# Attention loads reordered: v ahead of q and k, raw weights later, q scaled later in a round

## The chip, the cores and the metric

The kernel runs on one core of one Trainium2 chip. The metric is device time in microseconds (us), the median of several runs. The engines are TensorE (PE in the profile, its weight loads PEld), VectorE (DVE), ScalarE (ACT), GpSimd (POOL) and SyncE (SP), whose queue (SPq) issues every load and store here. Times in the profile count from the start of the profiled span.

## The reference, cut to what matters

Three stages follow one another: sparse attention over 4 batches and 8 heads, and two feed-forward layers on its output.

```python
# q, k, v: (4, 8, 576, 64)
scores = q @ k.T / 8
local   = (rel >= 0) & (rel < 32)                    # heads 0 to 3
strided = (rel >= 0) & (pos_k % 32 == pos_q % 32)    # heads 4 to 7
attn = softmax(where(mask, scores, -1e9))
x = (attn @ v)             # to (2304, 512)
h = x @ w_in               # (512, 2048)
x = (h * cos(h)) @ w_out   # (2048, 512)
x = (silu(x @ w_gate) * (x @ w_val)) @ w_out2        # d_ff 1536
```

The weights arrive in a wide type: a raw tile of 128 x 512 values is 512 KB and has to be converted to float32 (ACT and DVE) and scanned for its largest magnitude before it is split into two half-precision parts.

## The kernel before

Attention works on 16 units (a batch and a pair of heads), two at a time, one strided and one local. A unit has three groups of tiles; the groups of two units alternate, so a **round** of six steps treats two units, and the loop at L775 runs over steps k with i = 2 (k // 6) and g = k % 6. There are 48 groups and eight rounds. Group j has its scores and row maxima in step j (L784, L785), its exponentials one step later (L814, on ACT), its row sums (DVE) and its normalisation (`norm`, L456: a reciprocal on DVE, then a product on POOL) in step j + 2, its transposes and their evacuation in step j + 5 (PE, then ACT), its product with v in step j + 6 (`values`, L479) and its store into the activations in step j + 7 (`put`).

Each engine takes its instructions in the order in which the program emits them. In each step `pump` (L815) adds about one us of work on the weights, from step 5 on: a raw tile is widened on ACT (`g0`, L224), scanned (`g1`, L227), shifted (`g2`, L231) and completed on DVE (`g3`, L235). The first call of `pump`, in step 5, emits `g0` of raw tiles 0 and 1 on ACT ahead of everything of step 6, and `g0` of tile 2 follows in step 6. The freed tile is loaded again by `load_raw` (L158) with the next one of a fixed order: 16 tiles of w_in, then w_out. There are six raw buffers.

All loads stand in one queue, SP's. Ahead of the loop (L737 to L754) it holds q and k of units 0 and 1, four small constants, v of units 0 and 1, and then raw tiles mixed with q and k of units 2 to 5 and v of units 2 and 3. Inside the loop, in step g = 5 of a round, it gets q and k of the units three rounds on (L808) and then v of the next round (L812). q and k lie in one tile, and v of a strided unit is loaded by two transfers of 54 partitions (L408), of a local unit by one of 96 (L404).

q has to be scaled in place before the scores of its unit. That is `scale_q` (L413), one POOL instruction for each unit; it waits for the load of that unit's q and k, and all later POOL instructions stand behind it. It is emitted for the two units of the next round in steps g = 2 and g = 3 (L786), ahead of the step's `norm`. PE emits a small extra product (L437) in each group, on ones.

After the loop, the first layer starts (L1012) and works on with the converted weights; its own weight work is again emitted between its products.

Of the kernel before, what the change touches and what calls it, by code (L numbers as in the profile page):

```python
# [55 lines left out]
HEAD, HSHARE = 14, 0.8  # L56
RATE, MINLAG = 0.4, 2
RAW = 6
XM = 5
HOMES, LATE, UNIT = 24, 4, 16  # L60
W7S = 3
# [10 lines left out]
def is_local(p):  # L72
    return p < NPAIR // 2
# [6 lines left out]
def build(tc, qk_l, qk_s, v_l, v_s, w_in, w_out, w_gate, w_val, w_out2, mask_l, mask_s, eye32, eye16, out):  # L80
    nc = tc.nc
    wide = w_in.dtype != F32
    with ExitStack() as ctx:
# [65 lines left out]
        for k, a in MATS.items():  # L149
# [3 lines left out]
        order = deque([("in", j) for j in range(M1)] + [("out", j) for j in range(M1)] * 2  # L153
                      + [(mat, j) for mat in ("gate", "val") for j in range(M2)]
                      + [(mat, 2 * j + i) for j in range(NPR) for mat in ("gate", "val") for i in range(2)]
                      + [("out2", j) for j in range(M2)] * 2)

        def load_raw():  # L158
            if not order:
                return  # L160
            mat, i = order.popleft()
            src = MATS[mat][i]
            if wide:
                t = ring.tile([128, 512, 2], I32, name="raw", bufs=RAW)
                nc.sync.dma_start(out=t.rearrange("p n w -> p (n w)"), in_=src.bitcast(I32))
            else:
                t = ring.tile([128, 512], F32, name="raw", bufs=RAW)
                nc.sync.dma_start(out=t, in_=src)
            raw.setdefault((mat, i), deque()).append(t)
# [20 lines left out]
        def pump(share):  # L190

            credit[0] = min(credit[0] + share, max(share, 1.0))
            while fill and credit[0] > 0:
                step_fill()

        def need(key):
            while key not in emitted:
                step_fill()
# [191 lines left out]
        units = [(b, p) for b in range(NB) for p in (2, 0, 3, 1)]  # L390
        qk_t, v_t = {}, {}

        def load_qk(i):
            b, p = units[i]
            loc = is_local(p)
            qk_t[i] = ap.tile([128, QKW[loc]], F32, name="qkl" if loc else "qks", bufs=3)
            nc.sync.dma_start(out=qk_t[i], in_=(qk_l if loc else qk_s)[b, p % 2])

        def load_v(i):
            b, p = units[i]  # L400
            loc = is_local(p)
            if loc:
                v_t[i] = ap.tile([LW, LT, 128], F32, name="vl")
                nc.sync.dma_start(out=v_t[i], in_=v_l[b, p % 2])  # L404
            else:
                v_t[i] = v_pair[i // 2 % 2]
                for u in range(2):
                    nc.sync.dma_start(out=v_t[i][64 * u:64 * u + SW, SP * u:SP * u + SP, :], in_=v_s[b, p % 2, u])  # L408

        def bank():  # L410
            return pm.tile([128, 512], F32, name="bank")

        def scale_q(i):  # L413
            q = qk_t[i][:, 0:S if is_local(units[i][1]) else QP]
            nc.gpsimd.tensor_scalar(out=q, in0=q, scalar1=SCALE, scalar2=1.0, op0=ALU.mult, op1=ALU.mult)
# [145 lines left out]
        def up1(blk, m, ks=range(KC), c=None, spare=None):  # L561
            n = BLOCKS[blk][1]
            if m == 0 and not c:
                turn[blk] = prod(sx[blk][1], scale_w["in"][1], 1.0 / TWO_PI)
            if not c:
                b = bank() if spare is None else pacc.tile([128, 512], F32, name=f"acc{spare}")
                c = dict(n=n, ph=b[:, 0:n], blk=blk)
            project(c["ph"], wi[m], xs[blk], n, ks)
            return c

        def up1_a(c):
            n = c["n"]
            c["w"] = ring.tile([128, 512], F32, name="tb", bufs=4)[:, 0:n]
            nc.scalar.activation(out=c["w"].bitcast(I32), in_=c["ph"], func=AF.Identity, scale=turn[c["blk"]], bias=quarter)  # L574
# [27 lines left out]
        def fold_pieces(blk, scales, dst, spans):  # L602
            n = BLOCKS[blk][1]
            h = n // 2
            y = xy[blk]
            b11, b12, b21, b22 = (y[:, k:k + 2, t:t + h] for k in (0, 2) for t in (0, h))
            t1, t2 = (t.rearrange("p (k n) -> p k n", k=2)[:, :, 0:h] for t in spans)
            parts = [(0, b11), (1, b21), (2, b22), (4, t1), (5, t2), (6, t1), (3, t2)]

            def sub(out, a, b):  # L610
                nc.vector.tensor_tensor(out=out, in0=a, in1=b, op=ALU.subtract)

            sums = {0: lambda: sub(t1, b12, b11), 1: lambda: sub(t2, b22, t1), 5: lambda: sub(t1, b22, b12),
                    6: lambda: sub(t2, b21, t2)}

            def piece(k):
                if k == 0:
                    dst[blk] = ring.tile([128, 2, 7, 512], F16, name="xs")
                hl = [dst[blk][:, i].rearrange("p q (k n) -> p q k n", k=2)[:, :, :, 0:h] for i in range(2)]
                s = scales[blk][0]  # L620
                if k in sums:
                    sums[k]()
                if k < 7:
                    i, src = parts[k]
                    hi_part(hl[0][:, i], src, s)
                if k:
                    i, src = parts[k - 1]
                    lo_part(hl[1][:, i], src, s, hl[0][:, i])
            for k in range(8):
                yield (0.7 if k else 0) + (0.7 if k in sums else 0), lambda k=k: piece(k)  # L630
# [107 lines left out]
        load_qk(1)  # L738
        for t, a in ((id16, eye16), (ms, mask_s), (ml, mask_l), (id32, eye32)):
            nc.sync.dma_start(out=t, in_=a)  # L740
        load_v(0)
        load_v(1)
        load_raw()
        load_qk(2)
        load_raw()
        load_qk(3)
        load_raw()
        load_v(2)
# [2 lines left out]
        load_qk(4)  # L751
        load_raw()
        load_qk(5)
        load_raw()  # L754
        warm = bank()
        for _ in range(WARM):
            nc.tensor.matmul(out=warm, lhsT=ones16, rhs=hot, start=True, stop=True)
# [13 lines left out]
        def keep_warm():  # L771
            t = bank()[:, 0:4 * LW].rearrange("p (n w) -> p n w", w=LW)
            nc.tensor.matmul(out=t, lhsT=id16, rhs=ml, start=True, stop=True)

        for k in range(len(gs) + LAGS[3] + 1):  # L775
            def group(lag):
                return gs[k - lag] if 0 <= k - lag < len(gs) else None
            i, g = 2 * (k // 6), k % 6
            if group(LAGS[0]):
                group(LAGS[0]).sums()  # L780
            if group(LAGS[1]):
                group(LAGS[1]).transposes()
            if group(0):
                group(0).scores()  # L784
                group(0).top()  # L785
                if g in (2, 3) and i + g < len(units):  # L786
                    scale_q(i + g)
            begun = k - len(gs) - K0
            if 0 <= begun < 2 * EARLY:
                m = begun // 2  # L790
                if begun % 2 == 0:
                    need(("in", m))
                    early = up1(0, m, range(KC // 2))
                else:
                    up1(0, m, range(KC // 2, KC), early)
                    up1_a(early)
                    steps.append((0, m, early))
            elif not group(0):
                keep_warm()
            if group(LAGS[3]):  # L800
                group(LAGS[3]).put()
            if group(LAGS[1]):
                group(LAGS[1]).evac()
            if group(LAGS[2]):
                group(LAGS[2]).values()
            if group(0) and g == 5:
                for j in (i + 6, i + 7):
                    if j < len(units):  # L808
                        load_qk(j)
                for j in (i + 2, i + 3):  # L810
                    if i and j < len(units):
                        load_v(j)  # L812
            if group(1):
                group(1).exps()  # L814
            pump(PUMP if k >= KP else 0)  # L815
            if group(LAGS[0]):
                group(LAGS[0]).norm()

        attn.close()
        pacc = ctx.enter_context(tc.tile_pool(name="pacc", bufs=1, space=bass.MemoryType.PSUM))  # L820
# [149 lines left out]
        def urge(pieces, key=None):  # L970
            urgent.extend((c, f, key) for c, f in pieces)
# [40 lines left out]
        for blk in range(NBLK):  # L1012
            for m in range(M1):
# [6 lines left out]
                if m == 0:  # L1020
                    if blk:
                        need_urgent(("xs", blk))
                    if blk == NBLK - 1:
                        urge(fold_pieces(0, sy, ys, spans), ("ys", 0))
                if m == (2 if blk else XM) and blk + 1 < NBLK:
                    urge(scale_pieces(blk + 1, sx))
# [135 lines left out]
        for s, (blk, j) in enumerate(slots):  # L1162
            n = BLOCKS[blk][1]
            h = n // 2
            if s == 1:
                need(("out2", NPR - 1))
                for _ in range(RAW):
                    t = ring.tile([128, 512, 2] if wide else [128, 512], I32 if wide else F32, name="raw", bufs=RAW)
                    flat = t.rearrange("p n w -> p (n w)") if wide else t
# [152 lines left out]
```

## Time and profile before

| quantity | value |
|---|---|
| median of 3 runs | 902.8 us (899.58 to 903.82) |
| span of the profiled execution | 902.2 us |
| mean granted clock of TensorE | 0.979 |
| PE busy | 862.4 us (96%) |
| DVE busy | 691.8 us (77%) |
| ACT busy | 521.2 us (58%) |
| POOL busy | 199.3 us (22%) |

The profiled execution took its span, 902.2 us; nothing is shown around it. The attention loop takes about the first 113 us. A share of busy time is a mean over stages with different limits, so the stages are read one by one. In a timeline row the first two numbers are start and duration, and the bracket at its end gives the idle time before the first of its instructions and what ended it. A row with x12 merges twelve instructions. The granted clock is a share of full speed: 1.00 is 2.4 GHz and 0.50 is 1.2 GHz.

### The profile page before, as it was taken

How to read it: one execution, taken by the hardware profiler on the slowest of the kernel's cores; microseconds unless marked ns; L12 is line 12 of the kernel's file. 1: busy time of each engine (PE TensorE's matmuls, PEld its weight loads, DVE VectorE, ACT ScalarE, POOL GpSimd, SP SyncE). 2: the span in 40 equal slices, each digit the busy share in tenths (PEclk: the TensorE clock that was granted, in tenths of full speed). 3: DMA queues.
4: the chain of work that ended last, by engine and by line, in shares of the span. 5: the costliest groups of instructions: out<-in, count | busy, mean ns of one | idle time of the engine just before them, and what ended most of it. 6: DMA issues, size and time to landing. Idle time of an engine off the chain costs nothing.

```text
span 902.2 us, 18542 instructions
## 1 busy us (share of the span) xinstructions
PE 862.4 (96%) x7228; PEld 609.8 (68%) x7228; DVE 691.8 (77%) x1337; ACT 521.2 (58%) x1046; POOL 199.3 (22%) x253
## 2 busy tenths in 40 slices
PE   7999999989999979899999998899999999999998
PEld 4776644434444434455655686788888899999998
DVE  4797989896758999869988378857886776776672
ACT  4787988763445667547887355536444444544440
POOL 3342414121234656522322200000000000000000
PEclk8897999999999989999999999999999999999999
DMA  9997751568545675651645344657677687888894
GB/s 302 352 304 219 249 187 48 163 189 272 191 144 197 214 241 178 225 204 49 215 136 198 156 151 177 247 200 265 233 255 267 216 273 284 299 290 309 317 330 148
DMA packets 53512, 200.61 MB, mean 222 GB/s; under 512 B 5456, under 2 KB 16208, under 8 KB 49584
## 3 DMA queue, kind: packets, MB, share of 16 engines
q1 hardware_dynamic: 53424, 199.42, 64.8%
q8 instruction: 57, 0.93, 0.5%
q14 instruction: 31, 0.25, 0.1%
HBM read 175.41 MB, written 23.99 MB: 221 GB/s over the span
## 4 chain that ended last, share of the span: by engine, by line
PE 66%; DVE 10%; ACT 7%; DMA 6%; issue 6%; POOL 4%; SPq 0%; POOLq 0%; ACTq 0%; DVEq 0%
PE acc L693 14%; PE bank L541 10%; PE bank L543 10%; PE bank L542 10%; PE acc L541 5%; PE acc L543 5%; PE acc L542 5%; DMA vl<-v_l 3%; PE bank L435 2%; DVE arena L248 2%; POOL arena L915 2%; POOL arena L589 2%; PE po L488 2%; ACT arena L245 2%; DMA v_pair<-v_s 1%
## 5 line engine op out<-in xcount | busy, mean ns | idle before, releaser
L541 PE MATMUL bank<-xs,wi 128*128 128x256 f16 (+3 forms) x780 | 233.8, 300 | 22.1 <-DVE tb L584 9.1
L543 PE MATMUL bank<-xs,wi 128*128 128x256 f16 (+3 forms) x780 | 234.1, 300 | 0.0
L542 PE MATMUL bank<-xs,wi 128*128 128x256 f16 (+3 forms) x780 | 233.9, 300 | 0.0
L589 POOL TENSOR_TENSOR arena<-tb,arena 128x512 f16<-128x512 f32 (+1 forms) x80 | 91.7, 1148 | 240.6 <-ACT arena L588 205.7
L542 PEld LDWEIGHTS <-wi 128*128 128x128 f16 x880 | 86.2, 98 | 62.5 <-issue 30.2
L541 PE MATMUL acc<-arena 128*128 128x512 f16 (+1 forms) x320 | 114.7, 358 | 0.0
L542 PE MATMUL acc<-arena 128*128 128x512 f16 (+1 forms) x320 | 114.5, 358 | 0.0
L543 PE MATMUL acc<-arena 128*128 128x512 f16 (+1 forms) x320 | 114.5, 358 | 0.0
L541 PEld LDWEIGHTS <-wi 128*128 128x128 f16 x880 | 86.3, 98 | 38.4 <-issue 4.1
L543 PEld LDWEIGHTS <-wi 128*128 128x128 f16 x880 | 86.3, 98 | 35.6 <-issue 1.4
L693 PEld LDWEIGHTS <-arena 128*128 128x128 f16 x1080 | 100.7, 98 | 8.2
L678 POOL TENSOR_TENSOR wi<-tb 128x256 f32<-128x256 f32 (+1 forms) x30 | 20.2, 675 | 347.5 <-DVE tb L659 347.5
L663 ACT ACTIVATE arena<-tb 128x256 f16<-128x256 f32 (+3 forms) x59 | 28.9, 489 | 115.3 <-DVE tb L659 111.6
L574 ACT ACTIVATE tb<-bank,quarter,c 128x512 int32<-128x512 f32 (+1 forms) x75 | 54.4, 725 | 49.5 <-PE bank L543 36.9
L542 PEld LDWEIGHTS <-arena 128*128 128x128 f16 x600 | 58.8, 98 | 35.0 <-issue 2.5
L693 PE MATMUL acc<-arena 128*128 128x256 f16 (+1 forms) x702 | 82.0, 265 | 0.0
L543 PEld LDWEIGHTS <-arena 128*128 128x128 f16 x600 | 58.7, 98 | 33.0 <-issue 0.2
L541 PEld LDWEIGHTS <-arena 128*128 128x128 f16 x600 | 58.8, 98 | 32.8 <-ACT arena L588 0.3
L658 DVE SCALAR_TENSOR_TENSOR tb<-tb,arena 128x512 f32<-128x512 f32 (+1 forms) x60 | 38.0, 634 | 44.9 <-ACT tb L652 44.8
L588 ACT ACTIVATE arena<-tb 128x512 f16<-128x512 f32 (+1 forms) x80 | 46.5, 581 | 35.4 <-PE acc L543 32.4
L541 PE MATMUL bank<-xs,arena 128*128 128x256 f16 (+1 forms) x240 | 62.9, 262 | 1.7 <-DVE arena L1190 1.2
L543 PE MATMUL bank<-xs,arena 128*128 128x256 f16 (+1 forms) x240 | 62.9, 262 | 0.0
(146 smaller groups left out, 1734.5 us busy)
## 6 DMA issues: line engine op xcount, KB each, us to landing
wi<-w SPq DMA_DIRECT2D x20, 1792.0 KB
arena<-w SPq DMA_DIRECT2D x60, 576.0 KB, 5.3
raw<-w_out SPq DMA_DIRECT2D x56, 512.0 KB, 4.0
arena<-w SPq DMA_DIRECT2D x10, 1792.0 KB
raw<-w_gate SPq DMA_DIRECT2D x24, 512.0 KB, 4.6
raw<-w_val SPq DMA_DIRECT2D x24, 512.0 KB, 4.4
w<-arena SPq DMA_DIRECT2D x42, 256.0 KB, 2.1
raw<-w_in SPq DMA_DIRECT2D x16, 512.0 KB
```

Of the source, the lines that this page charges most:

```text
L245: nc.scalar.activation(out=dst, in_=src, func=AF.Copy, scale=s)
L248: nc.vector.scalar_tensor_tensor(out=dst, in0=src, scalar=s, in1=hi, op0=ALU.mult, op1=ALU.subtract)
L541: nc.tensor.matmul(out=o, lhsT=w[:, 0, c], rhs=x[0], start=first, stop=False, **kw)
L542: nc.tensor.matmul(out=o, lhsT=w[:, 0, c], rhs=x[1], start=False, stop=False, **kw)
L543: nc.tensor.matmul(out=o, lhsT=w[:, 1, c], rhs=x[0], start=False, stop=last, **kw)
L574: nc.scalar.activation(out=c["w"].bitcast(I32), in_=c["ph"], func=AF.Identity, scale=turn[c["blk"]], bias=quarter)
L588: nc.scalar.activation(out=g[:, 0, 0:n], in_=w, func=AF.Copy)
L589: nc.gpsimd.tensor_tensor(out=g[:, 1, 0:n], in0=w, in1=g[:, 0, 0:n], op=ALU.subtract)
L658: nc.vector.scalar_tensor_tensor(out=t, in0=t, scalar=1.0, in1=gate, op0=ALU.add, op1=ALU.mult)
L663: nc.scalar.activation(out=to, in_=src, func=AF.Copy, scale=2.0 ** -11)
L678: nc.gpsimd.tensor_tensor(out=t_sums[:, 0, 0:h], in0=c["t"][0][:, h:2 * h], in1=c["t"][0][:, 0:h], op=ALU.subtract)
L693: nc.tensor.matmul(out=o[:, c], lhsT=w[:, 256 * i + 128 * c:256 * i + 128 * c + 128], rhs=unit(u)[:, x:x + h], start=j == c == i == 0, sto ...
```

## The change

Four edits, all in the attention stage.

- `scale_q` for the next round moves from steps g = 2 and 3, ahead of `norm`, to the end of steps g = 4 and 5, behind `norm`.
- In step g = 5 the loads of v for the next round are issued ahead of those of q and k for three rounds on.
- In the loads ahead of the loop, q and k of unit 2 come ahead of v of units 0 and 1, and the raw tiles come later: the first stands behind q and k of unit 3 and three at the very end. Their number (six) is the same.
- `load_raw` holds back any w_out tile; from step 30 on, each step releases one, until none is held, and then loads go out as before.

```diff
--- before.py
+++ after.py
@@ -56,6 +56,7 @@
 HEAD, HSHARE = 14, 0.8
 RATE, MINLAG = 0.4, 2
 RAW = 6
+RELEASE = 30
 XM = 5
 HOMES, LATE, UNIT = 24, 4, 16
 W7S = 3
@@ -155,7 +156,22 @@
                       + [(mat, 2 * j + i) for j in range(NPR) for mat in ("gate", "val") for i in range(2)]
                       + [("out2", j) for j in range(M2)] * 2)
 
+        hold, held_back = [True], [0]
+
+        def release():
+            if held_back[0]:
+                held_back[0] -= 1
+                next_raw()
+            else:
+                hold[0] = False
+
         def load_raw():
+            if hold[0] and order[0][0] == "out":
+                held_back[0] += 1
+            else:
+                next_raw()
+
+        def next_raw():
             if not order:
                 return
             mat, i = order.popleft()
@@ -738,11 +754,9 @@
         load_qk(1)
         for t, a in ((id16, eye16), (ms, mask_s), (ml, mask_l), (id32, eye32)):
             nc.sync.dma_start(out=t, in_=a)
+        load_qk(2)
         load_v(0)
         load_v(1)
-        load_raw()
-        load_qk(2)
-        load_raw()
         load_qk(3)
         load_raw()
         load_v(2)
@@ -751,7 +765,8 @@
         load_qk(4)
         load_raw()
         load_qk(5)
-        load_raw()
+        for _ in range(3):
+            load_raw()
         warm = bank()
         for _ in range(WARM):
             nc.tensor.matmul(out=warm, lhsT=ones16, rhs=hot, start=True, stop=True)
@@ -783,8 +798,6 @@
             if group(0):
                 group(0).scores()
                 group(0).top()
-                if g in (2, 3) and i + g < len(units):
-                    scale_q(i + g)
             begun = k - len(gs) - K0
             if 0 <= begun < 2 * EARLY:
                 m = begun // 2
@@ -804,17 +817,21 @@
             if group(LAGS[2]):
                 group(LAGS[2]).values()
             if group(0) and g == 5:
+                for j in (i + 2, i + 3):
+                    if i and j < len(units):
+                        load_v(j)
                 for j in (i + 6, i + 7):
                     if j < len(units):
                         load_qk(j)
-                for j in (i + 2, i + 3):
-                    if i and j < len(units):
-                        load_v(j)
             if group(1):
                 group(1).exps()
             pump(PUMP if k >= KP else 0)
             if group(LAGS[0]):
                 group(LAGS[0]).norm()
+            if group(0) and g >= 4 and i + g - 2 < len(units):
+                scale_q(i + g - 2)
+            if k >= RELEASE:
+                release()
 
         attn.close()
         pacc = ctx.enter_context(tc.tile_pool(name="pacc", bufs=1, space=bass.MemoryType.PSUM))
```

## Rows read from the trace of the kernel before

**Rows 1.** The page's slices of the span, 40 equal ones: granted clock and DMA share.

```profile
PEclk8897999999999989999999999999999999999999
DMA  9997751568545675651645344657677687888894
```

**Rows 2.** Busy time by stage: stretch, PE, PEld, DVE, ACT, POOL, clock, DMA share, GB/s.

```profile
14.50:31.00 16.50, 15.98 (x149) 10.81 (x149) 8.66 (x23) 10.18 (x33) 5.47 (x10) 0.51 1.03 361
...
31.00:60.00 29.00, 29.00 (x491) 20.89 (x491) 27.43 (x76) 26.91 (x103) 12.94 (x20) 1.00 1.00 310
...
72.50:82.20 9.70, 9.70 (x96) 6.67 (x96) 4.98 (x13) 5.90 (x20) 2.51 (x4) 0.51 0.60 188
...
128.00:160.00 32.00, 31.82 (x150) 14.39 (x149) 30.32 (x57) 27.54 (x45) 13.64 (x13) 1.00 0.17 58
```

**Rows 3.** Timeline of POOL in the opening.

```profile
6.28 0.67 POOL L415 TENSOR_SCALAR qkl<-qkl 128x576 f32<-128x576 f32 x1 [0.80 <-DMA qkl<-qk_l]
13.32 0.69 POOL L415 TENSOR_SCALAR qks<-qks 128x594 f32<-128x594 f32 x1 [6.37 <-DMA qks<-qk_s]
```

**Rows 4.** Timeline of PE in the opening, the transposes of group 0.

```profile
14.57 0.69 PE L470 MATMUL tp<-id,e_s 128*128 128x128 f32 x2 [3.38 <-POOL e_s L459]
```

**Rows 5.** Timeline of ACT in the opening.

```profile
16.15 1.24 ACT L224 ACTIVATE wi<-raw 128x512 f32<-128x512 f32 x2
18.31 0.49 ACT L477 ACTIVATE pt<-tp 96x384 f32<-96x384 f32 x1 [0.92 <-PE tp L466]
```

**Rows 6.** The page's list of DMA issues, sizes of one transfer.

```profile
raw<-w_in SPq DMA_DIRECT2D x16, 512.0 KB
...
qks<-qk_s SPq DMA_DIRECT2D x8, 594.0 KB, 6.6
...
vl<-v_l SPq DMA_DIRECT2D x8, 432.0 KB, 4.7
...
v_pair<-v_s SPq DMA_DIRECT2D x16, 162.0 KB
```

**Rows 7.** Busy time, columns as in rows 2, of two stretches with different loads.

```profile
36.00:38.50 2.50, 2.50 (x40) 1.69 (x37) 2.40 (x6) 2.28 (x9) 0.46 (x1) 1.00 1.02 410
40.00:43.00 3.00, 3.00 (x47) 2.03 (x47) 2.97 (x7) 2.70 (x12) 2.37 (x3) 1.00 0.99 228
```

**Rows 8.** The chain that ended last: start, duration, what.

```profile
58.90 12.35 DMA v_pair<-v_s
```

**Rows 9.** Timeline of PE: scores and products with v, at either clock.

```profile
47.62 0.71 PE L435 MATMUL bank<-qkl 64*64 64x96 f32 x12
...
53.36 0.56 PE L435 MATMUL bank<-qks 64*64 64x54 f32 x12
...
71.29 0.56 PE L488 MATMUL po<-pts,v_pair 118*64 118x54 f32 x12 [0.79 <-DMA v_pair<-v_s]
...
72.40 1.23 PE L435 MATMUL bank<-qkl 64*64 64x96 f32 x12
...
82.17 0.56 PE L435 MATMUL bank<-qks 64*64 64x54 f32 x12
```

**Rows 10.** Timelines of POOL (`norm` in g = 4) and PE (scores in g = 0).

```profile
33.57 0.55 POOL L459 TENSOR_TENSOR e_s<-e_s,ls 128x216 f32<-128x216 f32 x1 [1.32 <-DVE ls L458]
...
96.25 0.55 POOL L459 TENSOR_TENSOR e_s<-e_s,ls 128x216 f32<-128x216 f32 x1 [1.17 <-ACT xy L510]
...
34.60 0.67 PE L435 MATMUL bank<-qks 64*64 64x54 f32 x16
...
96.89 0.67 PE L435 MATMUL bank<-qks 64*64 64x54 f32 x16
```

**Rows 11.** Busy time, columns as in rows 2, ahead of the second fall of the clock.

```profile
68.40:71.80 3.40, 2.19 (x38) 1.54 (x38) 3.15 (x8) 3.00 (x9) 1.09 (x2) 1.00 1.03 258
```

**Rows 12.** The raw tiles until 130 us: duration min/median/max, first and last start.

```profile
L165 SPq DMA_DIRECT2D raw<-w_out x22: 327/328/447, 55.6 to 126.1; - x22
...
L174 DVE TENSOR_REDUCE pw_out<-raw x16: 662/677/682, 90.8 to 125.4; 128x1 f32<-128x512 f32 x16
```

## Prediction

> **What bounds the kernel now.** I read the slices first, then busy time by stage, then the timelines around each place where the clock fell. In the slices the reader sees a busy PE nearly throughout, and TensorE's granted clock low in two places of the attention stage; the DMA engines are full for some 70 us and then ease [rows 1]. By stage, PE is busy all of 31 to 60 us at full clock with DVE at 27.43 of 29 us, so attention there goes at PE's pace with DVE close behind; behind attention, at 128 to 160 us, PE is busy 31.82 of 32 us and DMA has room [rows 2]. So time won in attention should come off the end nearly whole. What can be won lies in the two stretches at half clock, 14.5 to 31 and 72.5 to 82.2 us, where DVE and ACT wait for PE [rows 2].
>
> Each begins at a wait for a load. In the opening, POOL stands 6.37 us at the `scale_q` of unit 2, until its q and k land at 13.32 [rows 3]. `norm` of group 0 stands behind it, and PE, at the transposes of that group, is idle for 3.38 us and restarts at 14.57 [rows 4], at half clock. At 71.29 PE waits 0.79 us for v of unit 8 [rows 9], a load that took 12.35 us from issue, to 71.25 [rows 8]; then the clock falls again.
>
> **Term 1, v ahead of q and k.** In step g = 5 of round 3, v of units 8 and 9 stood behind q and k of units 12 and 13, and behind one w_out tile, issued at 55.6 us [rows 12]; the change takes both from ahead of it. A q and k pair is two tiles of some 594 KB, 1.21 MB, a raw tile 0.52 MB [rows 6]. Such loads run at 410 GB/s, against 228 GB/s in a stretch that mostly moves v [rows 7]. So v lands 1.21/0.410 + 0.52/0.410 = 4.2 us earlier, five times the 0.79 us that PE waited. In round 4 it gains as much or more. q and k then land later, but they are loaded three rounds, some 33 us, before their scores, so nothing is late for that.
>
> What goes if v is there: PE's scores of step 31 began at 72.40. From the products at 71.29, less 0.79 of wait, and with the transposes between them at full clock, they could begin near 71.15, which is 1.25 us earlier. Steps 31 to 34 then took 82.17 - 72.40 = 9.77 us; the same three steps two rounds earlier at full clock took 53.36 - 47.62 = 5.74 us [rows 9], so half clock cost 4.0 us. Together 5.2 us. Next late would be ACT, some 0.4 us ahead of the same products, which stays. Bounds: 1.2 us if the clock falls here all the same, 5.2 if not; I take 5.2, because 4.2 us of lead is far from the wait.
>
> The Trainium skill, "TensorE: Matmul & The Clock Gate", section Terms, prices throttled time at one minus the clock's share: half of these 9.77 us would be 4.9 us. The rows give 4.0, since the steps did not quite halve in speed, so the measurement decides; by the page the total would be 0.9 us better.
>
> **Term 2, the opening.** q and k of unit 1 are there at 6.28 [rows 3]. The sum of the loads from there, with 0.6 us for the constants, 3.4 us for a pair of v (0.77 MB at 228), 1.48 us for a q and k tile and 1.28 us for a raw tile (both at 410) [rows 6, 7], gives for unit 2 before: 6.28 + 0.6 + 3.4 + 1.28 + 1.48 = 13.0, and the row says 13.32 [rows 3]. The same sum for the new order: q and k of unit 2 at 8.4, v of units 0 and 1 at 11.8, q and k of unit 3 at 13.2, raw tile 0 at 14.5, v of units 2 and 3 at 17.9, raw tile 1 at 19.2, raw tile 2 at 22.0. So POOL no longer blocks `norm`, and PE's transposes of group 0 come at about 11.8 instead of 14.57.
>
> But there is a new wait. In step 5 ACT gets the widening of raw tiles 0 and 1, done at 17.39 before, and the evacuation of group 1 stands behind them, at 18.31 [rows 5]. With tile 1 landing at 19.2, or 0.5 us later if v runs slower, the widening ends at 19.9 to 20.4 and the evacuation at about 20.9; PE's product of group 1 waits for it. DVE's scan of tile 0 waits too, and through its reciprocal `norm` and then `scale_q` of unit 3 come at about 17.8, which holds PE's scores of step 7. So the 3.4 us of idle time at one place becomes some 5 us in three or four pieces, and step 8 begins at about 21.9 where it began at 24.35 before (14.57 plus three steps of 9.77/3 = 3.26 us). That is 2.4 us ahead. What it is worth depends on the clock. Before, the half clock held 16.5 us from the restart, the second time 9.8 us. Restarting at 21.0, it would hold to 37.5 or to 31.7. In the first case 15.6 us at 3.26 bring PE to step 12.8, which it reached at 31.0 + 2.8 x 1.91 = 36.3 before, 1.2 us earlier; in the second it is at step 11 at 31.7, against 32.8 before, 1.1 us won. If the clock never falls, ACT limits the gain to 3.3 us, because it has the delayed widenings to do and is busy 26.91 of 29 us anyway [rows 2]. So the bounds are a loss of 1.2 and a gain of 3.3. I take 0: gaps this long have brought the clock down before, and the two hold times lie on either side.
>
> **Term 3, q scaled later.** Before, the scaling came three or four steps ahead of its scores and cost nothing after the opening. Now it stands behind `norm` of step g = 4, and PE needs it two steps later. `norm` waits for a reciprocal that DVE reaches only after that step's row maxima and weight work. On the trace of before, `norm` of that step in round 1 starts at 33.57 and takes 0.55; with 0.69 for the scaling [rows 3] it would be done at 34.81, and PE wants the scores at 34.60: 0.21 us late. In round 6 it is 96.25 + 1.24 = 97.49 against 96.89, 0.60 late [rows 10]. The six rounds 1 to 6 come to 2.2 us (0.21 and 0.60 are the first and the last). The other unit's scaling, one step later, has the same distance; as the first wait has already put PE back, it mostly hides. Bounds: 0.5 us, if DVE, given time by each wait, loses its lag; 4.4 us, if the second scaling costs as much again. I take 2.2, straight from the rows.
>
> **Term 4, w_out held back.** The held tiles go out from step 30, near 70 us; the first scan of w_out stands at 90.8 us [rows 12], near 86 after the other terms. Three tiles take 3.8 us at 410 GB/s, and the queue by then is shorter by what was taken off it. Nothing: the cover is some 12 us, and without it each tile would cost 1.3 us. The new order adds no instruction; SP's queue has no new wait except that v's buffer is freed a little later in a step than that of q and k, which then stand behind v.
>
> **Sum.** 902.2 - 5.2 + 0 + 2.2 = 899.2 us on the profiled execution; the median of the runs stands 0.6 us above that execution, so 899.8 us.
>
> **The rivals.** A, the opening keeps its clock or gets it back soon: +3.3 us of gain, and with `scale_q` costing 1 us rather than 2.2 the time is 899.8 - 4.5 = 895.3 us. For it: PE restarts early, with shorter gaps than 3.38 us. Against it: several of them together.
>
> B, slower: the new waits for `scale_q` bring the clock down in the middle of attention. For it: before the second fall PE was busy 2.19 of 3.40 us [rows 11], so 1.2 us of idle time stood ahead of it; a round in which both scalings are late by 0.6 us each looks the same. The price of one fall is 4.0 us (three steps, as above) to 6.8 (16.5 us in steps of 3.26 instead of 1.91 us): 903.8 to 906.6 us for one fall, 907.8 to 913 us for two. It decides from the second fall on. Against it: most of the waits by the rows are below 0.6 us.
>
> The same page of the Trainium skill (section on why this matters for kernels) lets the clock fall after a gap in which PE does nothing, and by it waits of half a microsecond would never cost it, so rival B would have next to no chance. The trace disagrees: PE was busy for most of the stretch before the fall [rows 11].
>
> C, the change doesn't do what it says: the stage is bound by the loads, PE meets another late load instead, and terms 1 and 3 fall away together, as a scaling hides in a load's wait: 902.8 us. For it: DMA is full to 70 us [rows 1, 2]. Against it: v's new place is 4.2 us ahead, and all that is held back can wait.
>
> **How the numbers follow.** The forecast, 899.8 (896.5 to 902.5), has 0.45; A has 0.22; B 0.23, of which 0.12 for one fall and 0.11 for two; C 0.10. What a measurement can tell from no change is about 0.5%, 4.5 us, so faster means below 898.3. A lies there, and 0.16 of the forecast, when the opening wins a part: 0.38. Slower, above 907.3, is two falls: 0.11. The same is the rest, 0.51. The range is 893.5 to 908: A with the smallest POOL cost below, one fall or a cheap second one above.
>
> **What would show it.** Right: no DMA wait of PE for v in rounds 3 and 4, and the slices near 72 us at full clock; POOL's first `norm` near 11.3 us; ACT idle ahead of the widening of tile 1 until about 19; PE waiting for POOL's `scale_q` at the scores of g = 0, 0.2 to 0.6 us each. Wrong: a clock at 1.00 through 14 to 31 us (A), half clock in rounds 2 to 6 behind such a wait (B), or a new DMA releaser of PE (C).

## The result and the profile after

The changed kernel takes 905.85 us (median; 902.28 to 914.55) against 901.25 us for the kernel before in the same comparison. The ratio is 1.0059, with a 95% interval of 1.0039 to 1.0078: by the ratio 5.3 us slower. I had forecast 899.8 us, 3.0 us below the 902.8 us that I had for the kernel before.

The two profiled executions point the other way, 900.5 us after against 902.2 us before, and their mean granted clocks differ as well: 0.988 in the one and 0.979 in the other. In 92 runs of the kernel before that stood beside the experiments (seven slower ones, at a lower clock, are left out) the median clock is 0.984, in 18 of the changed kernel 0.9845. So my profile of before showed an execution with more half clock than most, and the profile of after one with less. Compared at the same clock, 0.989, eight runs of before span 897.6 to 898.6 us, and three of after 902.1 to 902.5 us: the loss is there without any difference in clock.

First the busy time by stage in the kernel after (stretch, then PE, PEld, DVE, ACT, POOL, granted clock, DMA share, GB/s), to be read against [rows 2]:

```profile
14.50:31.00 16.50, 11.41 (x139) 7.89 (x135) 9.35 (x26) 9.61 (x33) 3.33 (x6) 0.69 1.03 359
31.00:60.00 29.00, 26.79 (x443) 18.99 (x441) 26.74 (x71) 24.75 (x95) 12.80 (x21) 1.00 1.00 313
72.50:82.20 9.70, 8.73 (x148) 6.33 (x148) 7.99 (x23) 8.95 (x34) 3.79 (x7) 1.00 0.93 331
82.20:107.60 25.40, 23.85 (x402) 17.02 (x398) 22.91 (x66) 22.43 (x82) 10.11 (x17) 1.00 0.80 246
```

The last stretch in the kernel before:

```profile
82.20:107.60 25.40, 25.40 (x431) 18.33 (x430) 23.22 (x71) 23.89 (x89) 9.63 (x16) 1.00 0.79 247
```

At 72 us the clock stays at 1.00 where it was 0.51. But PE, which was busy all of 31 to 60 us, is now idle for 2.2 of these 29 us, and for 1.55 of the 25.4 us of the last stretch, where it was idle for none. What it waits for, from 31 to 115 us (total us, times, longest):

```profile
PE bank L451 <- POOL qkl L431: 3.3, 4, 1.3
PE bank L451 <- POOL qks L431: 1.7, 3, 0.7
PE bank L137 <- DVE tops L131: 0.6, 1, 0.6
PE po L504 <- ACT pt L493: 0.3, 1, 0.3
```

L431 is `scale_q`. The scores wait for it 5.0 us in all, and no wait for v is left. One round on DVE, POOL and PE (start, duration):

```profile
70.67 0.74 DVE L264 SCALAR_TENSOR_TENSOR xs<-xy,s,xs 128x512 f16<-128x512 f32 x1
...
71.92 0.96 DVE L264 SCALAR_TENSOR_TENSOR xs<-xy,s,xs 128x512 f16<-128x512 f32 x1
...
71.67 0.67 POOL L475 TENSOR_TENSOR e_l<-e_l,ls 128x288 f32<-128x288 f32 x1 [1.46 <-DVE ls L474]
72.30 1.11 POOL L431 TENSOR_SCALAR qkl<-qkl 128x576 f32<-128x576 f32 x1
...
73.47 0.71 PE L451 MATMUL bank<-qkl 64*64 64x96 f32 x12 [1.26 <-POOL qkl L431]
```

POOL is idle until DVE has its reciprocal (`ls`), then does `norm`, then the scaling, and PE has waited 1.26 us when that is done. The opening, on ACT, DVE, POOL and PE:

```profile
15.90 0.67 ACT L240 ACTIVATE wi<-raw 128x512 f32<-128x512 f32 x1 [3.12 <-DMA raw<-w_in]
21.05 0.67 ACT L240 ACTIVATE wi<-raw 128x512 f32<-128x512 f32 x1 [4.49 <-DMA raw<-w_in]
...
23.77 0.67 ACT L240 ACTIVATE wi<-raw 128x512 f32<-128x512 f32 x1 [0.99 <-DMA raw<-w_in]
...
15.90 0.69 DVE L243 TENSOR_REDUCE pw_in<-raw 128x1 f32<-128x512 f32 x1 [2.93 <-DMA raw<-w_in]
...
17.99 0.67 POOL L475 TENSOR_TENSOR e_l<-e_l,ls 128x288 f32<-128x288 f32 x1 [4.68 <-DVE ls L474]
18.62 0.67 POOL L431 TENSOR_SCALAR qkl<-qkl 128x576 f32<-128x576 f32 x1
...
11.07 0.44 PE L486 MATMUL tp<-id,e_s 128*128 128x128 f32 x2 [0.56 <-DVE mx L459]
...
19.34 1.23 PE L451 MATMUL bank<-qkl 64*64 64x96 f32 x12 [4.05 <-POOL qkl L431]
...
22.15 0.91 PE L504 MATMUL po<-pt,vl 96*64 96x64 f32 x12 [1.04 <-ACT pt L493]
```

PE's first transposes come at 11.07 instead of 14.57 [rows 4], but two longer waits follow. DVE stands still for raw tile 0 until 15.90, its reciprocal, `norm` and `scale_q` of unit 3 come behind that, and PE waits 4.05 us for the scaling. ACT stands still for raw tile 1 until 21.05, its evacuation comes behind that, and PE waits another 1.04 us. The 3.38 us of idle time have moved and grown.

### The profile page after: what moved, and what is told of

It reads as the page before. It is cut to its first block, busy times and chain, and to the rows that moved or that the text cites. A ratio compares the mean times of both kernels' runs of the same rounds, so it can differ in the third digit from the quotient of the medians.

```text
span 900.5 us, 18535 instructions
## 1 busy us (share of the span) xinstructions
PE 854.7 (95%) x7228; PEld 604.6 (67%) x7228; DVE 694.5 (77%) x1337; ACT 520.0 (58%) x1046; POOL 198.0 (22%) x253
## 4 chain that ended last, share of the span: by engine, by line
PE 67%; DVE 11%; ACT 8%; issue 5%; POOL 5%; DMA 4%; SPq 0%; POOLq 0%; ACTq 0%; DVEq 0%
PE acc L709 14%; PE bank L557 10%; PE bank L559 10%; PE bank L558 10%; PE acc L557 5%; PE acc L559 5%; PE acc L558 5%; PE bank L451 2%; DVE arena L264 2%; POOL arena L605 2%; PE po L504 2%; POOL arena L932 2%; ACT arena L261 2%; DMA raw<-w_in 1%; ACT arena L604 1%
```

## The experiments

All stood beside runs of the kernel before; the ratio is against these, so kernels of different comparisons are compared by their ratios. Theory S: `scale_q`'s new place costs, the rest gains. Its rival, theory L: the raw tiles that land late in the opening cost, and the scaling is hidden.

| kernel | median us | ratio to before | 95% interval |
|---|---|---|---|
| the whole change | 905.85 | 1.0059 | 1.0039 to 1.0078 |
| e1_scale_late | 906.55 | 1.0056 | 1.0029 to 1.0084 |
| e2_scale_back | 902.28 | 0.9985 | 0.9955 to 1.0015 |
| e3_v_first | 898.10 | 0.9963 | 0.9939 to 0.9986 |
| e4_first_loads | 903.28 | 1.0025 | 0.9999 to 1.0050 |
| e5_hold | 902.10 | 0.9988 | 0.9959 to 1.0017 |
| f3_one_step | 899.22 | 0.9974 | 0.9941 to 1.0006 |
| p1_ahead_of_norm | 899.70 | 0.9969 | 0.9938 to 1.0001 |
| f1_round0 | 900.20 | 0.9990 | 0.9967 to 1.0013 |
| f2_need_order | 903.63 | 1.0020 | 0.9989 to 1.0051 |
| g1_v_first_hold | 899.21 | 0.9975 | 0.9947 to 1.0003 |
| g2_old_loads_one_step | 898.92 | 0.9965 | 0.9933 to 0.9996 |

The runs of before in the first comparison of experiments (e1 to e4) have a median of 900.71 us, in the second (e5, f1 to f3) 902.05 us, in the third (p1, g1, g2) 902.84 us.

**The late scaling alone.**

```diff
 # in the kernel before
-                if g in (2, 3) and i + g < len(units):
-                    scale_q(i + g)
 ...
                 group(LAGS[0]).norm()
+            if group(0) and g >= 4 and i + g - 2 < len(units):
+                scale_q(i + g - 2)
```

> The kernel before with the late scale_q alone. Theory S (the late scale_q is what costs): PE waits for scale_q in rounds 1 to 6, 4 to 6 us in all, and the clock falls more often; the opening wins up to 3 us because POOL no longer stands ahead of norm. So 1 to 5 us slower than before (902 to 906). Theory L (the late raw tiles cost): scale_q is hidden, the opening wins, 2 to 4 us faster than before.

Measured: 0.56% slower, as much as the whole change. PE's waits from 31 to 115 us:

```profile
PE bank L435 <- POOL qkl L415: 2.3, 3, 1.3
PE bank L435 <- POOL qks L415: 2.0, 3, 0.7
PE bank L136 <- DVE tops L130: 0.6, 1, 0.6
PE po L488 <- ACT pt L477: 0.3, 1, 0.3
```

That is 4.3 us of waits for POOL without any of the new loads. Theory L, by which it should have been faster, falls. No wait for v stands in this list either, although v is still behind q and k here; more on that under term 1.

**The change without it.**

```diff
 # in the changed kernel
+                if g in (2, 3) and i + g < len(units):
+                    scale_q(i + g)
 ...
-            if group(0) and g >= 4 and i + g - 2 < len(units):
-                scale_q(i + g - 2)
```

> The changed kernel with scale_q back in steps g = 2 and 3, all loads as changed. Theory S: no PE wait for scale_q after round 0, 4 to 8 us faster than the changed kernel, so 2 to 4 us faster than before (897 to 899). Theory L: ACT still waits for raw tiles 1 and 2 until 21 and 24 us, the time stays within 2 us of the changed kernel (904 to 907).

Measured: 0.15% below before, interval across 1; some 6.7 us below the changed kernel by the two ratios. Its trace has no wait of PE for POOL from 31 to 115 us (it lists the same three waits as p1_ahead_of_norm below). The mechanism holds. The gain against before is less than expected; g1_v_first_hold, which differs from this kernel in the first loads alone, came out at 0.9975, so the new first loads would cost some 0.9 us of it, well within the noise.

**v first alone.**

```diff
 # in the kernel before, step g = 5
+                for j in (i + 2, i + 3):
+                    if i and j < len(units):
+                        load_v(j)
                 for j in (i + 6, i + 7):
                     if j < len(units):
                         load_qk(j)
-                for j in (i + 2, i + 3):
-                    if i and j < len(units):
-                        load_v(j)
```

> The kernel before with v ahead of q and k in the loop alone. My term 1: no DMA wait for v of unit 8, no fall of the clock near 72 us; up to 5 us faster, 896 to 900. If the kernel before seldom falls there in other runs, nothing: 900 to 902.

Measured: 0.37% faster, 3.3 us, the only single part that clearly wins. Busy time by stage and PE's wait:

```profile
14.50:31.00 16.50, 16.07 (x197) 10.97 (x199) 10.97 (x28) 12.33 (x44) 6.12 (x10) 0.71 1.03 362
60.00:72.50 12.50, 11.35 (x190) 8.02 (x186) 10.31 (x32) 11.34 (x42) 4.46 (x9) 1.00 0.95 283
72.50:82.20 9.70, 9.70 (x168) 7.05 (x167) 9.17 (x29) 8.32 (x33) 4.06 (x7) 1.00 0.97 264
...
67.79 0.56 PE L488 MATMUL po<-pts,v_pair 118*64 118x54 f32 x12 [0.44 <-DMA v_pair<-v_s]
```

PE's product starts 3.5 us earlier than in [rows 9], and still behind a wait, of 0.44 us. So v came 3.5 us earlier, and most of that was used up because PE was earlier too, the half clock of the opening having ended sooner. The prediction's lead of 4.2 us had left PE's own lead out. Where the 3.3 us come from this trace doesn't show: the median clock of its runs is 0.988, against 0.985 for those of before beside it, but runs without a profile don't tell where their half clock lay.

**The first loads alone.**

```diff
 # in the kernel before, ahead of the loop
+        load_qk(2)
         load_v(0)
         load_v(1)
-        load_raw()
-        load_qk(2)
-        load_raw()
         load_qk(3)
 ...
-        load_raw()
+        for _ in range(3):
+            load_raw()
```

> The kernel before with the new order ahead of the loop alone. Theory S: within 2 us of before, as the earlier q and k of unit 2 pays for the raw tiles that land 5 to 6 us later. Theory L: 3 to 5 us slower than before (904 to 906), with ACT idle until raw tiles 1 and 2 land.

Measured: 0.25% slower, 2.3 us, with the interval just reaching 1. It lies between the two theories' numbers. ACT and PE in its opening:

```profile
21.43 0.67 ACT L224 ACTIVATE wi<-raw 128x512 f32<-128x512 f32 x1 [4.35 <-DMA raw<-w_in]
...
15.44 0.88 PE L466 MATMUL tp<-id,e_l 128*96 128x128 f32 x3 [2.98 <-POOL e_l L459]
...
22.52 0.91 PE L488 MATMUL po<-pt,vl 96*64 96x64 f32 x12 [1.34 <-ACT pt L477]
...
57.23 0.33 PE L488 MATMUL po<-pts,v_pair 118*64 118x54 f32 x4 [0.55 <-DMA v_pair<-v_s]
58.49 0.56 PE L488 MATMUL po<-pts,v_pair 118*64 118x54 f32 x12 [0.93 <-DMA v_pair<-v_s]
```

The old wait comes back one group later (`scale_q` of unit 3 now stands ahead of `norm` of group 1), and ACT's is added. Later PE waits twice for v, 1.5 us in all, and the clock falls a second time:

```profile
60.00:63.00 3.00, 3.00 (x34) 1.88 (x31) 1.90 (x5) 1.21 (x6) 0.01 (x1) 0.53 0.99 370
```

So the 2.3 us are not all the opening's.

**w_out held back alone** (the lines of `release`, `next_raw` and the call from step 30 on, in the kernel before).

> The kernel before with w_out's raw tiles held back to step 30 alone. My term 4: nothing of its own; at most 1 us faster, as one tile of 1.3 us goes from ahead of v of unit 8: 899 to 902.

Measured: 0.12% below before, interval across 1. As expected, nothing that can be told.

**One step earlier.**

```diff
 # in the changed kernel
-            if group(0) and g >= 4 and i + g - 2 < len(units):
-                scale_q(i + g - 2)
+            if group(0) and g in (3, 4) and i + g - 1 < len(units):
+                scale_q(i + g - 1)
```

> The changed kernel with scale_q one step earlier: at the end of steps g = 3 and 4, still behind norm. Theory S says that the wait comes from the distance: norm ends some 1.4 steps behind PE's scores of its step, so two steps leave nothing over for the 0.69 us of scaling and three steps (1.9 us more) hide it whole. PE waits for scale_q only in the opening; 4 to 6 us faster than the changed kernel, 898 to 901, like e2_scale_back. If POOL's place behind norm itself were at fault, it would stay near 905.

**The same steps, ahead of `norm`.**

```diff
 # in the changed kernel
                 group(0).top()
+                if g >= 4 and i + g - 2 < len(units):
+                    scale_q(i + g - 2)
 ...
-            if group(0) and g >= 4 and i + g - 2 < len(units):
-                scale_q(i + g - 2)
```

> The changed kernel with scale_q in the same steps g = 4 and 5, but ahead of the step's norm (behind the row maxima, as in the kernel before). If the wait comes from standing behind a norm that waits for DVE's reciprocal, POOL does the scaling at once and PE waits for scale_q under 1 us in all in rounds 1 to 6: 898 to 901. If the step as such is too late, the waits of 4 to 5 us stay: 904 to 907.

Measured: both below before by 0.26% and 0.31%, each with an interval that just touches 1, and 0.85% and 0.90% below the changed kernel by the ratios. PE's waits from 31 to 115 us in the second (the first shows the same three):

```profile
PE acc L557 <- ACT xy L517: 0.6, 1, 0.6
PE bank L137 <- DVE tops L131: 0.6, 1, 0.6
PE po L504 <- ACT pt L493: 0.3, 1, 0.3
```

No wait for POOL is left in either. So the cost is neither POOL's work nor the step as such: it is that the scaling stands behind a `norm` that waits for DVE, with only two steps to go. One more step, or a place ahead of that `norm`, hides it whole.

**Better openings.** f1_round0 takes the old first loads and scales late in round 0 alone; f2_need_order puts the first loads in the order of their use, with the scaling of f3; g1_v_first_hold and g2_old_loads_one_step keep the old first loads, with v first and w_out held back, and scale as before or one step after (g = 3 and 4).

> The changed kernel with the old loads ahead of the loop, and scale_q late in round 0 alone (steps 4 and 5), in steps g = 2 and 3 afterwards. Theory S with the opening's part: POOL no longer stands ahead of norm of group 0 (the 3.1 to 3.4 us idle at PE go), ACT has its raw tiles at 11.4, 14.2 and 17.1 us, and v is early: 3 to 5 us below v first alone, 893 to 896. If the opening is bound by the loads whatever the order, it is as v first alone, 897 to 899.

> As f3_one_step, with the loads ahead of the loop in the order in which the opening needs them: q and k of unit 2, raw tiles 0 and 1, v of unit 0, q and k of unit 3, v of unit 1, three raw tiles, q and k of units 4 and 5, v of units 2 and 3, the last raw tile. ACT's first widenings end near 11, PE's idle time in the opening is under 2 us in all and the clock may not fall: 891 to 895. If the clock falls all the same: 895 to 898.

> The kernel before with v first in the loop and w_out held back, the first loads and scale_q as before: the two parts that cost nothing. As v first alone, 2 to 5 us faster than before (896 to 899).

> As g1_v_first_hold, with scale_q at the end of steps g = 3 and 4: POOL no longer stands ahead of norm of groups 0 and 1, so PE's idle time of 3.1 us before its first transposes goes. If the opening then runs into the next load (raw tiles, as in f1_round0), it is as g1, 897 to 899; if not, 893 to 896.

Measured: f1 0.10% below before, f2 0.20% above, both with 1 inside. Both missed what I expected: f1's median, 900.2 us, lies 1 us above the higher of the two ranges that I gave, and f2's, 903.6 us, 6 us above. In f1 ACT waits in turn for four raw tiles:

```profile
14.38 0.68 ACT L240 ACTIVATE wi<-raw 128x512 f32<-128x512 f32 x1 [1.04 <-DMA raw<-w_in]
18.09 0.69 ACT L240 ACTIVATE wi<-raw 128x512 f32<-128x512 f32 x1 [1.97 <-DMA raw<-w_in]
23.19 0.66 ACT L240 ACTIVATE wi<-raw 128x512 f32<-128x512 f32 x1 [1.73 <-DMA raw<-w_in]
27.40 0.66 ACT L240 ACTIVATE wi<-raw 128x512 f32<-128x512 f32 x1 [2.13 <-DMA raw<-w_in]
```

So what the opening gains at POOL it seems to meet again at the next load. In f2 PE's only long wait there is 1.99 us, and yet the clock, in the column before DMA share, was low for longer than in the profile after:

```profile
17.57 1.22 PE L451 MATMUL bank<-qkl 64*64 64x96 f32 x12 [1.99 <-POOL qkl L431]
...
14.50:31.00 16.50, 14.51 (x154) 10.22 (x152) 10.07 (x28) 10.16 (x38) 4.82 (x9) 0.58 1.02 304
31.00:60.00 29.00, 29.00 (x445) 20.61 (x441) 24.12 (x64) 23.38 (x91) 11.54 (x18) 0.88 1.02 299
```

g1 and g2 came out at 0.9975 and 0.9965, within what v first alone gives. v first alone, 898.1 us, is then the simplest version that beats both kernels; g2 beats both as well, and the runs do not tell them apart. Having v first doesn't end the waits for it: in g2 PE waits 1.9 us for v, near 103 us.

```profile
PE po L504 <- DMA v_pair<-v_s: 1.9, 2, 1.3
...
82.00:107.00 25.00, 23.03 (x359) 16.11 (x356) 20.97 (x62) 21.84 (x76) 8.86 (x15) 1.00 0.97 265
```

## Why the prediction was wrong, by its own steps

I forecast a gain of 3.0 us and measured a loss of 5.3 us. Of the 8.3 us between them, term 3 has 2.8 us by the waits of the trace and up to some 6 us by the ratios; terms 1 and 2 have the rest.

**Term 3 was mis-sized, and it is the largest part of the error.** I put the wait for `scale_q` at 2.2 us, by adding the lateness of the first scaling of each round and taking the second to hide behind it. The waits came to 5.0 us in the profile after. By the ratios, the late scaling costs 5.0 us in e1, and 6.7 to 8.1 us go when it is taken back or moved in the changed kernel (e2, f3, p1). The upper bound I gave, 4.4 us, was too low as well.

The step that failed is "it mostly hides". Where the first scaling was late, by 0.50, 0.71 and 0.54 us, the second did hide, but for 0.15 us. In the other three rounds the first was in time, so there was nothing to hide behind, and the second was late by 0.92, 1.26 and 0.92 us. Of the waits after, 3.3 us belong to the second unit (`qkl`) and 1.7 us to the first. The signs I gave named the scores of g = 0 alone; the longest waits stand at g = 1. Two of the seven waits after, one of each kind:

```profile
33.84 0.67 PE L451 MATMUL bank<-qks 64*64 64x54 f32 x16 [0.50 <-POOL qks L431]
48.01 0.71 PE L451 MATMUL bank<-qkl 64*64 64x96 f32 x12 [0.92 <-POOL qkl L431]
```

The trace of before had that in it: in round 2, `norm` of the second unit and a scaling of 0.67 us would end at 48.30, where PE began those scores at 47.62 [rows 9], 0.68 us late.

```profile
39.82 1.13 POOL L415 TENSOR_SCALAR qks<-qks 128x594 f32<-128x594 f32 x1
...
46.96 0.67 POOL L459 TENSOR_TENSOR e_l<-e_l,ls 128x288 f32<-128x288 f32 x1 [1.43 <-DVE ls L458]
```

Taking the later of the two in each round from that trace makes some 2.9 us (an estimate), still not 5.0. About 1.0 us more is the scaling's own time: four of the twelve took 0.84 to 1.11 us, against the 0.69 us that I had from [rows 3], and before the change, too, it could take 1.13 us, as the row at 39.82 shows. The one at 72.30 took 1.11 us beside a DVE instruction that reads two tensors, which took 0.96 us there and 0.74 us at 70.67 with POOL idle; the other three overlap such DVE instructions as well. The Trainium skill, "GPSIMD Engine Reference", section 1, says that GpSimd shares its SBUF interfaces with VectorE, with contention where a DVE instruction has two inputs in SBUF; these durations agree, though no run here separates other causes. The remaining 1.1 us are not explained. That DVE would catch up during the waits, my lower bound, did not come: from round 1 to round 6 they are 0.50, 0.92, 0.86, 1.26, 0.92 and 0.54 us.

**Term 1: the wait and the fall are gone, but that the order of the loads did it is not shown, and the size belonged to one execution.** The wait for v of unit 8 and the fall of the clock near 72 us are gone in the changed kernel, as said. They are gone in e1 and e5 as well, with v still behind q and k (60 to 82 us in e1, then in e5, which holds w_out back):

```profile
60.00:82.00 22.00, 20.05 (x331) 14.23 (x329) 18.89 (x54) 18.80 (x70) 8.35 (x13) 1.00 0.86 258
60.00:82.00 22.00, 21.41 (x359) 15.35 (x357) 19.75 (x58) 19.52 (x77) 9.02 (x16) 1.00 0.84 264
```

So the two profiles of before and after don't show that the order of the loads did it. Besides, 4.0 of the 5.2 us were the price of that fall, and the median run of before, at a clock of 0.984, has less half clock than the profiled one at 0.979: 0.005 of 902 us is 4.5 us of full clock, or some 9 us spent at half clock, about the second stretch of [rows 2]. That suggests, but doesn't show, that the median run has no second fall. The part is worth 3.3 us (1.3 to 5.5) in e3.

**Term 2 came as described, and later.** Raw tiles 0, 1 and 2 reached ACT at 15.90, 21.05 and 23.77 (I had 14.5, 19.2 and 22.0), and `scale_q` of unit 3 came at 18.6 instead of 17.8. Step 8 began at 23.79 instead of the 21.9 I had, 0.9 us ahead of before and not 2.4. I took the sum to be 0 and the loss at most 1.2 us. The runs do not settle it: e4, the loads alone, says a loss of 2.3 us, with an interval from nothing to 4.5, but it has waits of its own, for the early scaling and for v; the pairs e2 against g1 and f3 against g2, which differ in the first loads alone, give a loss of 0.9 and 0.8 us by their ratios, well inside their intervals.

**Term 4** was nothing, as said (e5).

The parts taken alone (e1, e3, e4, e5) make 5.0 - 3.3 + 2.3 - 1.1 = 2.9 us, and the whole measured 5.3 (3.5 to 7.0). With intervals of some 2.5 us on each part the two do not contradict each other, but the sum proves little; e4's waits for v show that the parts act on each other.

**Rival B named the right place and the wrong price.** Its time for one fall, 903.8 to 906.6 us, holds the measured 905.85 us, but by luck. The new waits did make the kernel slower, but not through the clock. In the profile after, the clock stands at 1.00 from 31 to 107 us through all of them, and the median clock of 18 runs is that of before. Ahead of the wait at 73.47 PE was as idle as ahead of the fall in [rows 11], and the clock did not fall:

```profile
70.07:73.47 3.40, 2.13 (x39) 1.41 (x37) 3.24 (x8) 3.40 (x14) 1.94 (x4) 1.00 0.90 246
```

So the idle time itself costs, in a stage that goes at PE's pace, and I should have put the case with all waits exposed (5 us or more of term 3, and term 1 at its smaller size) among the rivals. The rule of the Trainium skill, "TensorE: Matmul & The Clock Gate" (section on why this matters for kernels), warns of long gaps only and so gives short waits no power over the clock: the trace after agrees, and the traces of before and of e4 do not, where the clock fell behind waits of 0.79 and 0.93 us for v. In g2 it stayed at 1.00 through a wait of 1.3 us for v. Why it fell in some and not in the others stays open. Rival A did not come in the median, and C is refuted for the changed kernel: no wait for a load is left after the opening.

**The price of half clock** by the runs is lower than the one of the Trainium skill, "TensorE: Matmul & The Clock Gate", section Terms, once more. Eight runs of before at a clock of 0.989 have a median span of 898.0 us and five at 0.979 of 903.5: 5.5 us, where one minus the clock's share would make 9.0 us of that difference (0.010 of 902). That these runs differ in nothing but the clock is not shown: in e5, whose opening stayed long at half clock and which holds w_out back, PE doesn't wait for v, so a low clock may also save a wait.

## What to carry to other kernels

An instruction that is moved behind one that waits inherits that wait: before moving it, follow what the new neighbour waits for on the trace, for each of the instructions that are moved, and take the latest one in each round as the least that it costs (2.9 us here, where 5.0 came). One profiled execution can hold an event that other runs of the same kernel don't have; compare its clock with that of other runs before a term rests on it. A load that is moved ahead of another wins only what waits for it, and pays with what waits for the other: here v had three rounds of q and k to pass, while the first raw tiles were already next on ACT.

## What the runs showed of the hardware that I had not expected

The time at half clock after a fall in the opening varied widely although PE was busy throughout. In e5_hold, whose opening is that of the kernel before, it lasted past 31 us by far, where the profile of before was at full speed from there on [rows 2]:

```profile
14.50:31.00 16.50, 16.00 (x149) 10.81 (x149) 8.67 (x23) 10.16 (x33) 5.47 (x10) 0.50 1.03 357
31.00:60.00 29.00, 29.00 (x402) 20.45 (x400) 22.14 (x62) 22.37 (x83) 10.27 (x17) 0.77 0.87 270
```

With PE busy all of 31 to 60 us, a clock of 0.77 there means some 13 us more at half speed. Over 14.5 to 31 us, with the same code up to there, the clock was 0.51 in before and 0.71 in e3_v_first. What decides when it rises again was not tried. It may well make much of the spread between runs of one kernel, as their spans go with their clocks (898.0 us at 0.989 and 903.5 at 0.979, as above), but runs without a profile don't show where their half clock lay.
